# Layer 1 of a fused attention and four-matmul kernel by seven block products, with a new form of h - tanh(h)

## The chip, the cores and the metric

The kernel runs on one core of one Trainium2 chip. The metric is the device time in microseconds (us). The program's name for every instruction's line is a helper's (L215), so groups are told apart by engine, operation and shape. PE is TensorE, DVE VectorE, ACT ScalarE, POOL GpSimd, SP the engine that issues most plain DMAs.

## The reference

Sigmoid attention over 4 batches x 12 heads x 448 tokens x 64, then two feed-forward pairs on 1792 tokens, all in float32:

```
scores = q @ k.T / 8 - log(448);  x = sigmoid(scores) @ v     # -> (1792, 768)
h = x @ moe_w_in                  # layer 1, 768 -> 2048
g = h - tanh(h);  y = g @ moe_w_out        # layer 2, 2048 -> 768
b = y @ moe2_w_in                 # layer 3, 768 -> 2048
b = max(b, 0) + alpha * min(b, 0);  out = b @ moe2_w_out      # layer 4
```

## The kernel before

Matrix products are done in float16 with every operand split in a high and a low part: hi*hi + hi*lo + lo*hi, three matmuls for one (PASSES). A power of two, taken from the largest or the root mean square value (scale_of: a maximum over the free axis on DVE, over the partitions on POOL, then some ten tiny DVE instructions), scales activations into float16's range. A split is one high part (ACT or DVE) and one low part (DVE, `scalar_tensor_tensor`).

Weights come as 64-bit words. `words` turns a block of 128 x 768 into float32 by three DVE instructions, `to_scratch` splits it and stores high and low in DRAM through a POOL DMA, `fetch` loads it again through SP when PE needs it. 16 such blocks make a layer's weights.

Tokens go in two halves (sb 0 and 1) of 896 = 2 x 448. Layers 2 to 4 are done by Strassen's seven products on 2x2 blocks of weights and of activations, in the order SEQ = 1, 2, 6, 5, 7, 4, 3. `convert_quarter` makes from four blocks of weights (a quarter q of the layer) the seven sums that the products need (WSUM: by accumulating DMAs on POOL, or by DVE). `entry` makes the seven sums of activations ahead of layer 3, `exits` ahead of layers 2 and 4; `multiply_in` is one product of layer 3 (18 matmuls), `multiply_out` the seven of layers 2 and 4.

Layer 1 is a plain product: 16 blocks of output features (`product`) x two token halves, 36 matmuls each, half 1 behind half 0 by a lag. `convert` prepares its 16 blocks of weights. `bend` takes h - tanh(h) from PSUM: Tanh, then a polynomial in tanh(h)^2 (three Squares) for small h, and h - tanh(h) itself for large h, chosen by a threshold (Relu, `copy_predicated`), with the block's four PSUM reads on DVE and ACT; a last Square adds up the squares for the next scale.

The order of all instructions is written out by a planner (`Plan`): every piece of work has engines that can do it, a cost, a due time counted back from the end of PE's list, and a window; it fills each engine's in-order queue by due time. 51 slots of 128 x 896 float32 hold everything; the planner hands them out too. AHEAD, CHAIN, KEEP_*, WIN_*, LAG, SPARE_V are its parameters. PSUM is four pairs of banks.

Layer 2 of half 0 needs the scale of all its 16 blocks of h - tanh(h), and all four quarters of layer 2's weights soon after its start; layer 3 takes its quarters one after another.

Of the kernel before, what the change touches and what calls it, by code (L numbers as in the profile page):

```python
# [28 lines left out]
SW = 2.0 ** 9  # L29
ACT_EXP = 14  # L30
# [5 lines left out]
T2_MAX = 0.07960005252012954  # L36
POLY_A, POLY_B, POLY_C = 0.21126108783558653, 0.2731174600517137, 0.6519434161747253
# [192 lines left out]
def body(ctx: ExitStack, tc, qkd, vd, w1, w2, w3, w4, al, out):  # L230
# [8 lines left out]
               for m in (1, 2, 3) for pr in range(1, 8) for q in range(NQ)}  # L239
    scratch.update({u: dr_pool.tile([128, 2 * UC], F16, name=f"scr_{u}") for u in range(NU)})  # L240
# [4 lines left out]
    cst = sb_pool.tile([128, 4], F32, name="cst")  # L245
    mx = sb_pool.tile([128, 8, KF], F32, name="mx")
# [97 lines left out]
    def convert(i):  # L344
        name = f"sw:{i}"
        words(i, name, [("#scr", i - 2)] if i > 1 else ())
        to_scratch(i, name, SW)

    def convert_quarter(m, q):
# [43 lines left out]
        put(2, a12, turned)  # L393
# [8 lines left out]
    def scale_of(g, n, f0=1.0, f1=1.0, root=None, exp=ACT_EXP, sw=SW, unit=False, reads=()):  # L402
# [6 lines left out]
        def second(e):  # L409
            if root is None:  # L410
                V.tensor_scalar(c[:, 1:2], c[:, 1:2], 2.0 ** -100, None, ALU.max)
# [8 lines left out]
            V.tensor_scalar(c[:, 5:6], c[:, 2:3], 2.0 ** -exp / sw, f1, ALU.mult, ALU.mult)  # L420
            if unit:
# [4 lines left out]
                V.tensor_scalar(c[:, 7:8], c[:, 7:8], 0.5, None, ALU.mult)  # L426

        add("V", {"V": 1.3 + (0.9 if unit else 0.0)}, second, [(f"#sa{g}",), *reads], [(f"#sc{g}",)])

    def inv_of(g):  # L430
        return sc[:, g, 5:6]
# [46 lines left out]
    def values(g, u, cost):  # L478
# [19 lines left out]
        if u == 6:  # L498
            b, j = divmod(g, H // 4)
            name = f"sx{j},{b}"  # L500
            add("A", {"A": act(T2, True)}, lambda e: A.activation(two(slot(name)), full(3), AF.Copy),
                banks(3), whole(name))
# [8 lines left out]
    turn = [0]  # L511

    def product(fp, j, sb):

        k0 = turn[0] % 4
        turn[0] += 1
        p = pst[k0]
        bt = 2 * sb + j

        def x_of(k):  # L520
            return f"sX{k // 2},{bt}"

        for c in range(2):
            w = f"sW{2 * fp + c}"

            def f(e, c=c, w=w):
                wt = pair_of(slot(w)).rearrange("p a (k c) -> p a k c", k=UN)
                for k in range(KD):
                    x = hl(slot(x_of(k)))[:, :, (k % 2) * S:(k % 2 + 1) * S]
                    for n, (x1, x2) in enumerate(PASSES):  # L530
                        PE.matmul(p[:, c, 0:S], wt[:, x1, k], x[:, x2],
                                  start=k == 0 and n == 0, stop=k == KD - 1 and n == 2)

            reads = [(w, 0), *(r for k in range(KD) for r in parts(x_of(k), (0, 1)))]
            add("T", {"T": 18 * MM}, f, list(dict.fromkeys(reads)), [(f"ps{k0}", c)], lat=0.2)
        return k0

    def lagged(n, lag):
        seq, k = [], 0
        for j in range(n):  # L540
            while k < min(n, j + lag + j // 2):
                seq.append((k, 0))
                k += 1
            seq.append((j, 1))
        return seq

    def bend(fp, j, sb, k0):

        p = full(k0)
        iv = inv_of(sb)  # L550
        u, z, t = (f"s{x}{fp},{j},{sb}" for x in "uzt")
        gs = f"sG{sb},{fp // NQ},{j},{fp % NQ}"
        f = 2 * fp + j
        s1 = [(f"#sc{sb}",)]
        add("A", {"A": act(T2, True, 1)}, lambda e: A.activation(two(slot(t)), p, AF.Tanh, scale=iv),
            [*banks(k0), *s1], whole(t))
        add("A", {"A": act(T2)}, lambda e: A.activation(slot(u), slot(t), AF.Square), whole(t), whole(u))
        add("A", {"A": act(T2, ptr=1)},
            lambda e: A.activation(slot(z), slot(u), AF.Square, scale=POLY_A, bias=cst[:, 1:2]),
            whole(u), whole(z))  # L560
        add("A", {"A": act(T2, ptr=1)},
            lambda e: A.activation(slot(u), slot(u), AF.Relu, bias=cst[:, 2:3]), [], whole(u))
        add("V", {"V": vec(T2)},
            lambda e: V.scalar_tensor_tensor(two(slot(z)), two(slot(z)), POLY_C, p, ALU.subtract, ALU.mult),
            banks(k0), whole(z))
        add("A", {"A": act(T2, ptr=1)}, lambda e: A.activation(slot(z), slot(z), AF.Square, scale=iv), s1, whole(z))
        add("V", {"V": vec(T2, 1)},
            lambda e: V.scalar_tensor_tensor(two(slot(gs)), p, iv, two(slot(z)), ALU.mult, ALU.mult),
            [*banks(k0), *whole(z), *s1], whole(gs))
        add("V", {"V": vec(T2, 1)},  # L570
            lambda e: V.scalar_tensor_tensor(p, p, iv, two(slot(t)), ALU.mult, ALU.subtract),
            [*whole(t), *s1], banks(k0))
        add("V", {"V": vec(T2, 1)},
            lambda e: V.copy_predicated(two(slot(gs)), two(slot(u)).bitcast(I32), p),
            [*banks(k0), *whole(u)], whole(gs))
        add("A", {"A": act(T2, ptr=1, acc=True)},
            lambda e: A.activation(slot(z), slot(gs), AF.Square, scale=sc[:, sb, 6:7],
                                   accum_out=mx[:, 2 + sb, f:f + 1]),
            [*whole(gs), *s1], [*whole(z), (f"mx{2 + sb}", f)])
        if f == KF - 1:  # L580
            scale_of(2 + sb, KF, sc[:, sb, 6:7], sc[:, sb, 7:8], 1.0, ACT_EXP2, SW2, reads=s1)
            exits(sb, 2 + sb, "G", "Q", MOVED[0])

# [4 lines left out]
    def entry(sb):  # L588
        g = 4 + sb

        def y(e):
            return f"sy{e},{sb}"

        def h(name, k):
            return two(slot(name))[:, k]

        def t23(c):
            return f"sT{c},{sb}"

        def t4(c):  # L600
            return f"sF{c // 2 * 2},{sb}"

        def sub(out_, a, b):
            add("V", {"V": vec(S)}, lambda e: V.tensor_tensor(h(*out_), h(*a), h(*b), ALU.subtract),
                [a, b], [out_])

        for c in range(3):
            sub((t23(c), 0), (y(c + 3), 1), (y(c), 1))
            sub((y(c), 1), (y(c), 1), (y(c), 0))
            sub((t23(c), 1), (y(c + 3), 1), (y(c), 1))  # L610
            split_act(f"sO15{c},{sb}", y(c), g, window=WIN_O)
# [366 lines left out]
```

## Time and profile before

| | us |
|---|---|
| median of 3 runs | 932.58 (932.17 to 932.75) |
| the profiled execution | 931.04 |
| its span, first to last instruction | 929.3 |
| PE busy | 916.1 |
| DVE busy | 776.2 |
| ACT busy | 632.6 |
| POOL busy | 122.6 |

Busy time is the union of an engine's instructions; the mean of a group includes what overlaps with its neighbours. A window's row gives the busy time of each engine within it. Idle time ahead of a group is put down to the engine that released it.

### The profile page before, as it was taken

Reading aid. Unit: us, or ns where it says so; the run is one execution under the profiler, and the core shown is the slowest. Engines: PE = TensorE matmul, PEld = TensorE weight load, DVE = VectorE, ACT = ScalarE, POOL = GpSimd, SP = SyncE. Lnnn points to the kernel's source line nnn. Section 1 sums busy time; section 2 is a strip of 40 time slices with the busy share of each in tenths; the row PEclk is TensorE's granted clock in tenths of the full one; section 3 lists DMA queues with packets and bytes.
Section 4 is the critical chain, followed back from the end, with each engine's and each line's share of the span. In section 5 each row is a group of like instructions: output and inputs, shape, how many; then the busy total and the mean of one; then the engine's idle time right before and its main releaser. Section 6 shows DMA issues by size and latency. Waiting matters only on the chain.

```text
span 929.3 us, 13532 instructions
## 1 busy us (share of the span) xinstructions
PE 916.1 (99%) x5136; PEld 450.6 (48%) x5136; DVE 776.2 (84%) x961; ACT 632.6 (68%) x814; POOL 122.6 (13%) x207
## 2 busy tenths in 40 slices
PE   7999999999999998999999999999999999999998
PEld 2333335555555554555555555555555455555554
DVE  6788769999988999998989997798999999974300
ACT  7889869999989998645555746876773577433300
POOL 0011210123120102000023232201210000000000
PEclk9999999999999999999999999999999999999999
DMA  9983753579381337755399999867665555453431
GB/s 351 412 288 138 247 197 120 171 238 288 119 233 54 122 119 199 242 171 207 110 330 295 368 363 347 273 203 269 241 237 204 203 189 182 149 175 117 148 121 61
DMA packets 57314, 197.51 MB, mean 213 GB/s; under 512 B 7200, under 2 KB 10528, under 8 KB 57248
## 3 DMA queue, kind: packets, MB, share of 16 engines
q0 software_dynamic: 21248, 99.10, 32.5%
q1 hardware_dynamic: 36000, 97.54, 30.6%
q8 instruction: 40, 0.66, 0.3%
q14 instruction: 26, 0.21, 0.1%
HBM read 139.21 MB, written 44.83 MB: 198 GB/s over the span
## 4 chain that ended last, share of the span: by engine, by line
PE 96%; DVE 1%; ACT 1%; DMA 1%; issue 0%; SPq 0%; ACTq 0%
PE ps L215 96%; DVE slot L215 1%; ACT slot L215 1%; DMA slot<-qk 1%; DVE ps L215 0%; SPq L215 0%; ACTq L215 0%
## 5 line engine op out<-in xcount | busy, mean ns | idle before, releaser
L215 PE MATMUL ps<-slot,slot 128*128 128x448 f16 (+2 forms) x4560 | 863.3, 369 | 3.5 <-DVE slot L215 2.3
L215 PEld LDWEIGHTS <-slot 128*128 128x128 f16 (+2 forms) x4752 | 430.4, 98 | 435.7 <-issue 33.2
L215 ACT ACTIVATE slot<-slot,sc 128x896 f16<-128x896 f32 (+1 forms) x185 | 187.6, 1032 | 70.4 <-PE ps L215 34.7
L215 ACT ACTIVATE slot<-slot 128x896 f32<-128x896 f32 (+4 forms) x211 | 185.7, 895 | 72.2 <-DVE slot L215 55.6
L215 DVE SCALAR_TENSOR_TENSOR slot<-slot,sc,slot 128x896 f16<-128x896 f32 (+1 forms) x146 | 161.6, 1137 | 30.8 <-ACT slot L215 30.6
L215 DVE SCALAR_TENSOR_TENSOR slot<-slot,slot 128x768 f16<-128x768 f32 (+2 forms) x125 | 120.2, 971 | 22.1 <-ACT slot L215 18.3
L215 DVE SCALAR_TENSOR_TENSOR slot<-stage,slot 128x768 int32<-128x768 int32 x128 | 120.6, 951 | 1.0
L215 POOL DMA_DIRECT2D scr<-slot x100 | 57.8, 583 | 300.3 <-DVE slot L215 207.2
L215 ACT ACTIVATE slot<-ps 128x896 f32<-128x896 f32 (+1 forms) x76 | 59.3, 792 | 50.9 <-PE ps L215 44.2
L215 DVE SCALAR_TENSOR_TENSOR slot<-ps,sc,slot 128x896 f32<-128x896 f32 (+1 forms) x50 | 48.3, 978 | 54.2 <-PE ps L215 30.8
L215 DVE TENSOR_TENSOR slot<-slot,slot 128x896 f32<-128x896 f32 (+2 forms) x98 | 92.9, 974 | 0.3
L215 ACT ACTIVATE slot<-ps,cst 128x896 f32<-128x896 f32 x84 | 79.6, 1014 | 7.9 <-PE ps L215 7.7
L215 ACT ACTIVATE slot<-ps,sc 128x896 f32<-128x896 f32 (+1 forms) x56 | 46.9, 839 | 55.4 <-PE ps L215 55.3
L215 POOL DMA_DIRECT2D stage<-w x60 | 35.1, 585 | 253.9 <-DVE slot L215 218.7
L215 ACT ACTIVATE slot<-slot,cst 128x896 f32<-128x896 f32 x64 | 66.4, 1038 | 1.8 <-DVE slot L215 0.6
L215 PE MATMUL ps<-slot 64*128 64x448 f16 (+1 forms) x576 | 57.4, 359 | 5.7 <-ACT slot L215 5.6
L215 DVE SCALAR_TENSOR_TENSOR slot<-slot,nalpha,slot 128x448 f32<-128x448 f32 x64 | 41.6, 677 | 10.9 <-ACT slot L215 10.8
L215 DVE TENSOR_TENSOR slot<-ps,slot 128x896 f32<-128x896 f32 (+1 forms) x42 | 36.8, 884 | 5.7 <-PE ps L215 3.9
L215 DVE TENSOR_SCALAR slot<-stage 128x768 int32<-128x768 int32 x64 | 35.0, 556 | 6.7 <-PE ps L215 3.6
L215 ACT ACTIVATE junk<-slot 128x448 f16<-128x448 f32 (+1 forms) x36 | 25.4, 706 | 20.4 <-DVE slot L215 19.9
L215 POOL DMA_DIRECT2D slot<-slot x32 | 29.3, 925 | 75.3 <-DVE slot L215 48.2
L215 PEld LDWEIGHTS ps<-slot,slot 128*64 128x64 f32 (+1 forms) x384 | 20.1, 135 | 38.6 <-issue 36.4
(21 smaller groups left out, 190.8 us busy)
## 6 DMA issues: line engine op xcount, KB each, us to landing
slot<-scr SPq DMA_DIRECT2D x184, 384.0 KB, 3.7
stage<-w POOLq DMA_DIRECT2D x60, 768.0 KB, 6.3
scr<-slot POOLq DMA_DIRECT2D x100, 384.0 KB, 5.2
slot<-slot POOLq DMA_DIRECT2D x32, 384.0 KB, 7.9
slot<-qk SPq DMA_DIRECT2D x23, 448.0 KB, 9.1
slot<-v SPq DMA_DIRECT2D x12, 448.0 KB, 9.0
out_t<-slot SPq DMA_DIRECT2D x24, 224.0 KB, 2.0
stage<-w SPq DMA_DIRECT2D x4, 768.0 KB, 11.3
```

Of the source, the lines that this page charges most:

```text
L215: return lambda *args, **kw: self.tc.keep_in_program_order(f(*args, **kw))
```

## The change

- Layer 1 goes by the seven products too. `layer_in` is now one loop for layers 1 and 3: for each half, for each quarter, the products 1, (4 and 3 of the quarter before), 2, 6, 5, 7. Half 0 is finished before half 1 starts. The weights of layer 1 are made by `convert_quarter` (28 scratch blocks in place of 16; WSUM[0] is False, its sums are on DVE), and its activations by `entry(0, sb)`, whose additions go through accumulating DMAs on POOL (MOVED[0] is True). Weights of layer 1 are fetched once for each half.
- h leaves PSUM into a slot: `copy_h` (ACT) after product 1, 6, 7 or 4, `finish_h` (DVE) adds products 2, 3 or 5. `bend` then works on the slot: for small h, h times the square of arctan(1.103 tanh(0.520 h)), for large h, h - tanh(h). The threshold can go to ACT or DVE.
- Off-diagonal blocks are kept with the other sign, so that the sums before the products are additions into a block in place (`join`, `plus`); the signs are put in by copies with scale -1 and by subtractions.
- For layer 4's scale the sums of the two Relus' outputs and the largest alpha stand in for the sum of squares (`relu_b`, `steepest`), and 32 Squares of layer 3 go.
- The planner's parameters are others.

```diff
-AHEAD = {1: (0, 1, 3, 0), 2: (19, 22, 0, 20), 3: (27, 50, 7, 42)}
-CHAIN = {1: 5, 2: 1, 3: 4}
-MOVED = (False, False)
-LAG, KEEP_W, KEEP_F, KEEP_P, WIN_F, WIN_O, WIN_P, SPARE_V, WIN_Q = 4, 6, 4, 7, 16, 31, 39, 12, 51
-WSUM = (True, True, False)
+AHEAD = {0: (23, 20, 16, 16), 1: (0, 16, 12, 25), 2: (41, 32, 35, 15), 3: (0, 60, 25, 0)}
+CHAIN = {0: 7, 1: 3, 2: 5, 3: 7}
+MOVED = (True, False, False, False)
+KEEP_W, KEEP_F, KEEP_P, WIN_F, WIN_O, WIN_P, SPARE_V, WIN_Q = 7, 5, 12, 14, 43, 29, 8, 16
+WSUM = (False, True, True, False)
+PACE = (2, 3)
...
+    def bend(sb, i, j, q):
+        h, u, t = (f"s{x}{sb},{i},{j},{q}" for x in "hut")
+        z = f"sG{sb},{i},{j},{q}"
...
+        add("A", {"A": act(T2)}, lambda e: A.activation(slot(z), slot(h), AF.Tanh, scale=G_IN), whole(h), whole(z))
+        add("A", {"A": act(T2)}, lambda e: A.activation(slot(z), slot(z), AF.Arctan, scale=G_MID), (), whole(z))
+        add("A", {"A": act(T2)}, lambda e: A.activation(slot(z), slot(z), AF.Square, scale=G_OUT), (), whole(z))
+        def large(e):
+            if e == "A":
+                A.activation(slot(u), slot(z), AF.Relu, bias=cst[:, 2:3])
+            else:
+                V.tensor_scalar(slot(u), slot(z), G_MAX, None, ALU.is_gt)
+        add("AV", {"A": act(T2, ptr=1), "V": vec(T2, fast=True)}, large, whole(z), whole(u))
+        add("V", {"V": vec(T2)}, lambda e: V.tensor_tensor(slot(z), slot(z), slot(h), ALU.mult), whole(h), whole(z))
+        add("A", {"A": act(T2)}, lambda e: A.activation(slot(t), slot(h), AF.Tanh), whole(h), whole(t))
+        add("V", {"V": vec(T2)},
+            lambda e: V.tensor_tensor(slot(t), slot(h), slot(t), ALU.subtract), whole(h), whole(t))
+        add("V", {"V": vec(T2)},
+            lambda e: V.copy_predicated(slot(z), slot(u).bitcast(I32), slot(t)), [*whole(u), *whole(t)], whole(z))
...
+    def copy_h(sb, i, j, q, k0):
...
+        add("A", {"A": act(T2, True, 1)}, lambda e: A.activation(two(slot(name)), full(k0), AF.Copy, scale=iv),
+            [*banks(k0), (f"#sc{sb}",)], whole(name))
+    def finish_h(sb, i, j, q, k0):
...
+        add("V", {"V": vec(T2, 1)},
+            lambda e: V.scalar_tensor_tensor(two(slot(name)), full(k0), iv, two(slot(name)), ALU.mult, ALU.add),
+            [*banks(k0), (f"#sc{sb}",)], whole(name))
+        bend(sb, i, j, q)
...
+    def plus(out_, a, moved):
+        if moved:
+            add("G", {"G": 0.9, "M": 0.45},
+                lambda e: G.dma_start(out=half(*out_), in_=half(*a), accum_op=ALU.add), [a], [out_], lat=5.0)
...
+        for c in range(3):
+            s0, s1 = (f"sx{c},{2 * sb}", f"sx{c},{2 * sb + 1}") if m == 0 else (f"sy{c},{sb}", f"sy{c + 3},{sb}")
+            got = {}
+            if m == 0:
+                got.update(operand(f"sO{m},a{c},{sb}", s0, 1, 2))
+                plus((s0, 0), (s1, 0), MOVED[m])
+                got[5] = alone(c, s0)
+                plus((s1, 0), (s1, 1), MOVED[m])
+                got.update(operand(f"sO{m},c{c},{sb}", s1, 7, 3))
+                plus((s0, 0), (s1, 1), MOVED[m])
+                plus((s0, 1), (s0, 0), MOVED[m])
...
+            got.update(operand(f"sO{m},d{c},{sb}", s0, 6, 4))
...
-    def squares(name, into, g, col):
-        add("A", {"A": act(T2, acc=True)},
-            lambda e: A.activation(slot(into), slot(name), AF.Square, scale=SQ, accum_out=mx[:, g, col:col + 1]),
-            whole(name), [*whole(into), (f"mx{g}", col)])
+    def relu_b(out_, src, scale, sb, place, reads, ps):
+        add("A", {"A": act(T2, ps, acc=True)},
+            lambda e: A.activation(two(slot(out_)), src(), AF.Relu, scale=scale,
+                                   accum_out=mx[:, 6 + sb, place:place + 1]),
+            reads, [*whole(out_), (f"mx{6 + sb}", place)])
...
+    for m in range(4):
+        for q in range(NQ):
+            convert_quarter(m, q)
+    def layer_in(m, copied, finished, last, ended):
+        tail = []
+        for sb in range(2):
+            for q in range(NQ):
+                yk, xk, zk = q % 2, 2, 3
...
+                multiply_in(m, 1, sb, q, yk, True)
+                copied(sb, 0, 0, q, yk)
+                if tail:
+                    tail.pop(0)()
+                multiply_in(m, 2, sb, q, xk, True)
+                finished(sb, 0, 0, q, xk)
+                if tail:
+                    tail.pop(0)()
+                multiply_in(m, 6, sb, q, yk, False)
+                copied(sb, 0, 1, q, yk)
+                multiply_in(m, 5, sb, q, zk, True)
+                multiply_in(m, 7, sb, q, yk, False)
+                copied(sb, 1, 1, q, yk)
+                finished(sb, 1, 1, q, zk)
+                tail = [fourth, third]
...
+    for sb in range(2):
+        scale_of(sb, KD, root=SQ, unit=True)
+        entry(0, sb)
+    layer_in(0, copy_h, finish_h, last_h, ended_h)
     for sb in range(2):
         second_layer(sb)
+        scale_of(4 + sb, 2 * KD, 1.0, inv_of(2 + sb), SQ, reads=[(f"#sc{2 + sb}",)])
+        entry(2, sb)
+    layer_in(2, copy_b, finish_b, last_b, ended_b)
     for sb in range(2):
         fourth_layer(sb)
```

## Rows read from the trace of the kernel before

**Rows 1.** The page's busy time, share of the span and instructions of each engine.
```profile
PE 916.1 (99%) x5136; PEld 450.6 (48%) x5136; DVE 776.2 (84%) x961; ACT 632.6 (68%) x814; POOL 122.6 (13%) x207
```

**Rows 2.** Timeline of PE: start, length, count, idle time before with its releaser.
```profile
353.64 372.61 PE L215 MATMUL ps<-slot,slot 128*128 128x448 f16 x1968 [2.34 <-DVE slot L215]
727.26 197.96 PE L215 MATMUL ps<-slot,slot 128*128 128x448 f16 x1044 [1.00 <-ACT slot L215]
```

**Rows 3.** Windows: stretch, length, busy (instructions) per engine, clock, DMA share, GB/s.
```profile
core 0: us, PE busy (x) PEld busy (x) DVE busy (x) ACT busy (x) POOL busy (x), PEclk, DMA share, GB/s
0.00:11.50 11.50, 5.83 (x40) 2.19 (x41) 4.74 (x7) 7.25 (x10) 0.34 (x7) 1.00 0.82 291
...
11.50:60.00 48.50, 48.50 (x378) 16.40 (x379) 39.41 (x50) 40.92 (x49) 3.44 (x6) 1.00 0.96 375
60.00:127.50 67.50, 67.50 (x530) 22.56 (x528) 52.95 (x76) 60.24 (x73) 11.93 (x22) 1.00 0.62 217
...
542.00:640.00 98.00, 98.00 (x520) 50.69 (x518) 82.20 (x116) 69.78 (x96) 18.90 (x30) 1.00 0.84 283
...
200.00:270.00 70.00, 70.00 (x372) 36.21 (x371) 68.36 (x74) 67.90 (x85) 16.03 (x25) 1.00 0.68 204
11.50:443.50 432.00, 429.66 (x2563) 200.26 (x2563) 390.68 (x466) 363.41 (x452) 60.15 (x100) 1.00 0.61 204
131.60:349.00 217.40, 217.40 (x1151) 112.45 (x1150) 207.50 (x240) 203.31 (x247) 33.64 (x55) 1.00 0.50 158
```

**Rows 4.** Groups by form, whole span, PE: count | busy us, mean ns | idle before.
```profile
L215 PE MATMUL ps<-slot,slot 128*128 128x448 f16 x4176 | 790.8, 352 | 3.5 <-DVE slot L215 2.3 <-ACT slot L215 1.0
```

**Rows 5.** The same groups, whole span, DVE and ACT.
```profile
L215 ACT ACTIVATE slot<-slot,sc 128x896 f16<-128x896 f32 x120 | 121.2, 1035 | 67.5 <-PE ps L215 34.7 <-DMA out_t<-slot 12.1 <-DVE slot L215 10.7
...
L215 ACT ACTIVATE slot<-slot 128x896 f32<-128x896 f32 x112 | 105.5, 946 | 30.5 <-DVE slot L215 27.2 <-DMA slot<-slot 2.0
...
L215 ACT ACTIVATE slot<-slot,cst 128x896 f32<-128x896 f32 x64 | 66.4, 1038 | 1.8 <-DVE slot L215 0.6
...
L215 ACT ACTIVATE slot<-slot,sc 128x896 f32<-128x896 f32 x64 | 65.9, 1033 | 2.9 <-DVE slot L215 2.6
...
L215 ACT ACTIVATE slot<-slot 128x768 f16<-128x768 f32 x75 | 62.0, 836 | 25.2 <-DVE slot L215 15.4 <-issue 5.6 <-DMA slot<-slot 1.3
...
L215 DVE COPY_PREDICATED slot<-slot,ps 128x896 f32<-128x896 int32 x32 | 37.9, 1185 | 0.1
...
L215 DVE SCALAR_TENSOR_TENSOR ps<-ps,sc,slot 128x896 f32<-128x896 f32 x32 | 36.8, 1150 | 0.0
...
L215 DVE SCALAR_TENSOR_TENSOR slot<-ps,sc,slot 128x896 f32<-128x896 f32 x32 | 36.7, 1146 | 5.3 <-ACT slot L215 4.8 <-issue 0.3
...
L215 DVE SCALAR_TENSOR_TENSOR slot<-slot,ps 128x896 f32<-128x896 f32 x32 | 34.4, 1075 | 0.2 <-ACT slot L215 0.2
...
L215 ACT ACTIVATE slot<-ps,sc 128x896 f32<-128x896 f32 x32 | 31.9, 995 | 5.3 <-PE ps L215 5.3
...
L215 DVE TENSOR_TENSOR slot<-slot,slot 128x768 f32<-128x768 f32 x16 | 15.1, 951 | 0.1
...
L215 DVE TENSOR_SCALAR slot<-slot 128x896 f16<-128x896 f32 x17 | 10.6, 623 | 4.5 <-DMA slot<-qk 2.6 <-PE ps L215 1.7
...
L215 ACT ACT_TABLE_LOAD x1 | 1.3, 1283 | 0.7 <-PEq L970 0.7
```

**Rows 6.** Groups of DVE by form, from 0 to 443.5 us.
```profile
L215 DVE SCALAR_TENSOR_TENSOR slot<-stage,slot 128x768 int32<-128x768 int32 x68 | 64.3, 951 | 0.6
...
L215 DVE SCALAR_TENSOR_TENSOR slot<-slot,sc,slot 128x896 f16<-128x896 f32 x49 | 54.1, 1141 | 4.3 <-ACT slot L215 4.2
...
L215 DVE SCALAR_TENSOR_TENSOR slot<-slot,slot 128x768 f16<-128x768 f32 x46 | 43.4, 950 | 7.9 <-ACT slot L215 5.0 <-PE ps L215 2.2
...
L215 DVE TENSOR_TENSOR slot<-slot,slot 128x896 f32<-128x896 f32 x29 | 30.5, 1080 | 0.0
```

**Rows 7.** Timeline of DVE at the start of layer 1.
```profile
137.42 5.39 DVE L215 SCALAR_TENSOR_TENSOR slot<-slot,sc,slot 128x896 f16<-128x896 f32 x5
```

More of the change, by code (lines that the diff above doesn't have):

```diff
@@ L500, in values @@
             name = f"sx{j},{b}"
-            add("A", {"A": act(T2, True)}, lambda e: A.activation(two(slot(name)), full(3), AF.Copy),
-                banks(3), whole(name))
+            for i in range(2):
+                add("A", {"A": act(S, True)},
+                    lambda e, i=i: A.activation(two(slot(name))[:, i], p[:, i, 0:S], AF.Copy,
+                                                scale=float(sign_of(i, b % 2))),
+                    [("ps3", i)], [(name, i)])
             col = 2 * j + b % 2
@@ L538, in lagged @@
[L538 to L582, printed above, removed]
@@ L630, in f, with multiply_in @@
+    def multiply_in(m, pr, sb, q, k0, fresh):
+        p = pst[k0]
+        w = f"sv{m},{pr},{q},{sb}"
+        fetch((m, pr, q), w)
+        mine = [ops[m, sb, pr, c] for c in range(3)]
         def f(e):
@@ L639, in f, with copy_b @@
                                   skip_group_check=True)
-        add("T", {"T": 18 * MM}, f, [(w, 0), *(x for name, half in mine for x in parts(name, (half,)))],
+        add("T", {"T": 18 * MM}, f, [(w, 0), *(x for name, k in mine for x in parts(name, (k,)))],
             banks(k0), lat=0.2)
-    def copy_of(k0, name):
-        add("A", {"A": act(T2, True)}, lambda e: A.activation(two(slot(name)), full(k0), AF.Copy),
+    def copy_b(sb, i, j, q, k0):
+        name = f"sB{sb},{i},{j},{q}"
+        add("A", {"A": act(T2, True)},
+            lambda e: A.activation(two(slot(name)), full(k0), AF.Copy, scale=float(sign_of(i, j))),
@@ new lines, in finish_b, with total @@
+    def finish_b(sb, i, j, q, k0):
+        a, b = f"sB{sb},{i},{j},{q}", f"sb{sb},{i},{j},{q}"
+        plain = sign_of(i, j) > 0
+        def total(e):
+            if plain:
+                V.tensor_tensor(two(slot(a)), full(k0), two(slot(a)), ALU.add)
+            else:
+                V.tensor_tensor(two(slot(a)), two(slot(a)), full(k0), ALU.subtract)
+        add("V", {"V": vec(T2)}, total, banks(k0), whole(a))
+        place = 2 * (4 * q + 2 * i + j)
+        relu_b(b, lambda: two(slot(a)), -1.0, sb, place, whole(a), False)
+        relu_b(a, lambda: two(slot(a)), 1.0, sb, place + 1, (), False)
+        f0 = 2 * q + i * KF // 2
+        if plain:
+            leak(a, b, a, f0, ALU.add, nalpha)
+        else:
+            leak(a, a, b, f0, ALU.subtract, alpha)
@@ L770, in copied @@
         def copied(bk, row, j, last):
-            add("A", {"A": act(S, True)}, lambda e: A.activation(y_half(row, j), bank(bk), AF.Copy),
+            add("A", {"A": act(S, True)},
+                lambda e: A.activation(y_half(row, j), bank(bk), AF.Copy, scale=float(sign_of(row // 3, j))),
                 [region(bk)], [(f"sy{row},{sb}", j)])
@@ new lines, in last_h, with last_b, ended_h @@
+    def last_h(sb, i, j, q, k0):
+        copy_h(sb, i, j, q, k0)
+        bend(sb, i, j, q)
+    def last_b(sb, i, j, q, k0):
+        a, b = f"sB{sb},{i},{j},{q}", f"sb{sb},{i},{j},{q}"
+        place = 2 * (4 * q + 2 * i + j)
+        relu_b(b, lambda: full(k0), -1.0, sb, place, banks(k0), True)
+        relu_b(a, lambda: full(k0), 1.0, sb, place + 1, banks(k0), True)
+        leak(a, b, a, 2 * q + i * KF // 2, ALU.subtract, alpha)
+    def ended_h(sb):
+        scale_of(2 + sb, KF, sc[:, sb, 6:7], sc[:, sb, 7:8], reads=[(f"#sc{sb}",)])
+        exits(1, sb, "G", "Q")
@@ L853, in body, with ended_b @@
+    def ended_b(sb):
+        scale_of(6 + sb, 2 * KF, 1.0, inv_of(4 + sb), None, ACT_EXP2 + 1, reads=[(f"#sc{4 + sb}",), ("amax",)])
+        exits(3, sb, "B", "P")
     for sb in range(2):
         scale_of(sb, KD, root=SQ, unit=True)
-        for j in range(KD // 2):
-            for b in range(2 * sb, 2 * sb + 2):
-                split_act(f"sX{j},{b}", f"sx{j},{b}", sb)
-    for q in range(NQ):
-        convert_quarter(1, q)
-    got = set()
-    for n, sb in lagged(KF, LAG):
-        fp, j = divmod(n, 2)
-        for u in (2 * fp, 2 * fp + 1):
-            if u not in got:
-                got.add(u)
-                fetch(u, f"sW{u}")
-        bend(fp, j, sb, product(fp, j, sb))
```

288 lines of the change are left out of this document (115 added, 173 removed).

## The prediction, made before the result was known

> **What bounds the kernel now.** I read the page's busy shares first: TensorE (PE) is busy in 99% of a 929.3 us span, VectorE (DVE) in 84%, ScalarE (ACT) in 68% [rows 1]. Then PE's timeline: from 125.37 us to the end it runs in three blocks, and the idle time ahead of the second and the third is 2.34 us (waiting for DVE, at the start of layer 2) and 1.00 us (waiting for ACT, in layer 3) [rows 2]. Before the blocks stands the attention stage, which PE also fills from about 11.5 us on. So a product that is left out shortens the span, as long as DVE and ACT deliver operands at the new speed. The third view is busy time by stretch [rows 3]: in layer 1 (131.6 to 349) DVE has 207.5 of 217.4 us and ACT 203.3, that is 94.5% together; from 200 to 270 they have 68.36 and 67.90 of 70, or 97.3%. In layer 3 ACT has slack (69.8 of 98). So the stretch to watch is the one up to the second half of layer 2, where all of layer 1's elementwise work has to be done. PE's pitch comes from the 200-to-270 row: 70.00 us for 372 matmuls, 0.188 us each.
>
> **TensorE.** Layer 1 before is 32 products of 36 matmuls, 1152; after it is 7 products x 4 quarters x 2 halves x 18 = 1008, like layers 2 to 4 (1152 + 3 x 1008 = 4176, the count of [rows 4]). 144 x 0.188 = 27.1 us go. The 2.34 us wait at layer 2 goes too: it waits for the exit of token half 0, whose last product now stands 94 us (504 x 0.188) ahead of layer 2. I leave the 1.00 us. The sum against the profiled execution's own 931.04 us: 931.04 - 27.1 - 2.3 = 901.6 if no new wait comes. The profiled execution is 1.5 us under the median 932.58, so 903.1 in the metric.
>
> **What DVE and ACT get.** All rows are of [rows 5] unless named.
> - Weights of layer 1: 28 scratch blocks in place of 16. 12 more low parts on DVE x 0.950 [rows 6] = 11.4 us, 12 more high parts (ACT at 0.836) = 10.0; and 16 sums of 0.951 = 15.2 on DVE, since layer 1's sums are not sent to the DMA.
> - Operands of layer 1: 10.5 full-size splits per half in place of 6, 9 more in all: 9 x 1.141 [rows 6] = 10.3 on DVE, 9 x 1.035 = 9.3 on ACT. Their additions go to 24 accumulating DMAs on POOL's queue.
> - The bend, 32 times. ACT before: 0.995 + 0.946 + 2 x 1.038 + 2 x 1.033, in sum 194.7 us (the short read of each sum stays). After: a scaled copy out of PSUM (0.995), Tanh, Arctan, Square, Tanh (four of 0.946) and the summed Square (1.033): 186.0. The threshold is one more, on ACT (1.038, 33.2 in all) or on DVE (nearest row 0.623, 19.9); I take ACT. DVE before: 1.075 + 1.146 + 1.150 + 1.185, 145.8; after: 24 x 1.146 and 32 x (2 x 1.080 [rows 6] + 1.185), 134.6.
> Arctan is in no row; I take Tanh's or Square's length, one pass over 896 elements (bounds 0.946 and 1.038, the nearest forms: 3 us apart over 32).
> Sum of the rows: DVE 11.4 + 15.2 + 10.3 - 11.2 = +25.7; ACT 10.0 + 9.3 - 8.7 + 33.2 = +43.8; together 69.5 us. Neighbouring instructions overlap: five low parts of 1.14 take 5.39 us, so the pitch is 1.06, 0.93 of the row [rows 7]. 69.5 x 0.93 = 64.6 us of engine time.
>
> **Where it must fit.** The second half of layer 2 can start only when all bends, all weights of layers 1 and 2 and the exit of half 0 are done. Before, by 443.5 us, the two engines had been busy for 395.4 and 370.7 us (0 to 11.5 plus 11.5 to 443.5 [rows 3]), 766 together. Of that some was ahead of need: two of the 34 weight blocks converted (68 word operations, 46 low parts), five of the 49 operand splits with four high parts on ACT, and the 13 block sums of half 1 out of 29 [rows 6]: 4 x 0.951 + 2 x 0.950 + 5 x 1.141 + 13 x 1.080 + 4 x 1.035 = 29.6, x 0.93 = 27.5. Needed after: 766 - 27.5 + 64.6 = 803 us of two engines. The point itself stands at 353.64 + 492 x 0.188 = 446.2 before; without new waits at 446.2 - 29.4 = 416.8. 803 of 2 x 416.8 is 96.3%, against 83% before. That is as dense as the densest stretch of the trace, over the whole time, attention included, where the two engines had 205.5 of 255 us (80.6%) up to 127.5. So it doesn't quite fit, and PE will wait there, or in pieces ahead of it.
> How much: in the attention stage the extra weight work has PE's time to fill, and I put the share half way between 80.6 and 97.3%, at 89%, 227 us. The other 576 us then run at the mean of 94.5 and 97.3%, 95.9%: 576 / 1.918 = 300.3 us, so 427.8, 11.0 us late. At 97.3% it is 423.5 (6.7 late), at 94.5% 432.3 (15.5 late), and with no better attention stage and 94.5% 443.6 (26.8 late). At 97.3% throughout there is no wait. Ends of the unknown: 0 and 27; I take 11. 931.04 - 29.4 + 11.0 = 912.6, 914 in the metric.
>
> **What costs nothing.** In layer 3 the 32 Squares (0.946 each) go and 64 Relus take over the sum: ACT is at 71% there and PE at 100%, so it gains nothing. The exits' blocks in another order, the signs folded into copies and sums, the bound from alpha and the extra scale factor are a handful of short instructions early or beside busy PE: 0, and 2 us if they fell into a start of a layer. SP's queue gets 40 more fetches of 384 KB in layer 1, one per product of 3.4 us, the rate at which layer 3 runs without waiting at a DMA share of 0.84; layer 1 has 0.50 before [rows 3]. POOL's queue is in order, so an accumulating DMA that waits for x holds the weight loads and stores behind it; POOL is busy 13%, and the loads stand a block ahead. Bounds 0 and 3 us, I take 0; uncovered, a late fetch would cost its product's wait. If the wait stays, late next is the exit of half 1: its reduce, its first splits, then PE.
> TensorE's clock: it is at full (2.4 GHz) in every stretch here, that around the 2.34 us wait included [rows 3]. The Trainium skill (TensorE: Matmul & The Clock Gate, the part on the clock gate) says that a pause that is long enough throws the engine back to 1.2 GHz. By that, a wait in one piece would also slow matmuls after it, some us on top; no run here shows it yet. The sum goes without it.
>
> **Rivals.**
> 1. It fits (wait under 5 us): 901 to 908, by the row 903. For it: 200 to 270 shows both engines at 97% together, and h now leaves PSUM by one copy, so PE no longer waits for a whole bend. Against: it asks that of 400 us. Chance 0.24.
> 2. The forecast, a wait of 5 to 19 us: 908 to 922. Chance 0.45.
> 3. A wait of 19 to 27 us: 922 to 930.6, still faster. Chance 0.11. A wait of 27.5 to 31.3 us is no change: 0.04.
> 4. Slower, by overload at the middle of layer 2: the two engines hold only the share that they had from 11.5 to 443.5, 754 of 864 us or 87.3% [rows 3]. 576 / 1.746 = 329.9, so 457.4, 40.6 late: 944. It decides from 576 / (2 x (289.3 + 29.4)), under 90.4% after 127.5. For it: the in-order engines must take a copy out of PSUM between two products, 3.4 us, as they now don't have to. Against: layer 1 holds 94.5% before. Chance 0.13.
> 5. Arctan is not in the table that is loaded. The trace has one table load of 1.28 us for Sigmoid, Tanh, Square, Relu and Copy [rows 5]. If Tanh and Arctan took turns, 64 loads are 82 us more on ACT: (576 + 82) / 1.918 = 343, 470.6, 54 late: 957. Chance 0.03.
> The Trainium skill (ScalarE: Activation LUTs, Table sets: the hidden batching unit) lists sigmoid, tanh and arctan in one set. By that there is no load; no row shows Arctan.
>
> **How the numbers follow.** A measurement tells 0.2% (1.9 us) from no change. Faster: 0.24 + 0.45 + 0.11 = 0.80; same 0.04; slower 0.13 + 0.03 = 0.16. The range goes from 899 (no wait, some of the 1.00 us and the layer starts gained too) to 935, where a wait of 32 us ends: above it lies most of rivals 4 and 5, some 0.13, below it some 0.03.
>
> **What would show it.** 4032 matmuls of 128x128 with layer 1 ending about 27 us earlier; one table load; DVE and ACT both above 93% from layer 1's start to the middle of layer 2; PE's new idle time in layer 1 or at the middle of layer 2, released by DVE or ACT; 112 scratch stores in place of 100. The forecast is wrong if PE's idle time there stays under 5 us or passes 19, if it stands in layers 3 and 4, or if PE waits for DMA fetches.

## The result, and the profile after

The changed kernel takes 905.36 us (median of 4, 904.37 to 905.45), the kernel before 932.66 in the same measurement (932.17 to 932.95). The ratio is 0.9705, with a 95% interval of 0.9689 to 0.9722: faster by 27.3 us. The forecast was 914, so the direction and the removed matmuls were right and the new wait was too large: the work fits, as rival 1 (901 to 908) had it.

The profiled execution took 904.37 us, its span is 902.6. Busy time of the changed kernel, and the clock in its 40 slices (the page's first two parts):

```profile
PE 889.6 (99%) x4992; PEld 436.9 (48%) x4992; DVE 794.3 (88%) x1002; ACT 637.6 (71%) x879; POOL 156.4 (17%) x243
...
PEclk9999999999999999999999999999999999999999
```

It answers to [rows 1]: PE has 26.5 us less, DVE 18.1 more, ACT 5.0 more, in a span that is 26.7 shorter. PE's timeline (start, length, count, idle time before with its releaser) answers to [rows 2]:

```profile
315.95 37.80 PE L213 MATMUL ps<-slot,slot 128*128 128x448 f16 x199 [1.42 <-ACT slot L213]
354.33 94.18 PE L213 MATMUL ps<-slot,slot 128*128 128x448 f16 x497 [0.57 <-DVE slot L213]
449.25 250.07 PE L213 MATMUL ps<-slot,slot 128*128 128x448 f16 x1320 [0.74 <-DVE slot L213]
700.32 77.61 PE L213 MATMUL ps<-slot,slot 128*128 128x448 f16 x408 [1.01 <-ACT slot L213]
```

The 2.34 us wait is gone. New are 1.42 us (at the end of layer 1, ACT's copy), 0.57 and 0.74 us (both in layer 2, DVE); the 1.01 us in layer 3 is the old one. The three new ones add up to 2.73 us. The windows (stretch, length, busy time and instructions of each engine, clock, DMA share, GB/s) answer to [rows 3]:

```profile
core 0: us, PE busy (x) PEld busy (x) DVE busy (x) ACT busy (x) POOL busy (x), PEclk, DMA share, GB/s
0.00:11.50 11.50, 6.57 (x48) 2.95 (x48) 4.85 (x7) 7.68 (x10) 0.32 (x6) 1.00 0.82 292
11.50:60.00 48.50, 48.50 (x376) 16.20 (x368) 45.88 (x59) 44.80 (x59) 8.78 (x16) 1.00 0.97 373
60.00:127.50 67.50, 67.50 (x530) 22.63 (x528) 66.43 (x98) 66.51 (x88) 24.09 (x34) 1.00 0.98 326
...
511.00:605.00 94.00, 94.00 (x499) 48.62 (x498) 93.23 (x135) 59.55 (x96) 19.88 (x32) 1.00 0.83 289
...
127.50:416.00 288.50, 286.50 (x1518) 147.27 (x1515) 284.56 (x346) 265.96 (x354) 62.21 (x90) 1.00 0.83 258
200.00:270.00 70.00, 70.00 (x372) 36.21 (x371) 70.00 (x81) 69.22 (x90) 17.97 (x26) 1.00 0.88 262
11.50:416.00 404.50, 402.50 (x2418) 186.10 (x2411) 396.87 (x501) 377.27 (x499) 95.09 (x139) 1.00 0.87 283
```

Look at DVE first: it is busy 66.43 of 67.5 us in the second part of the attention stage, 70.00 of 70 from 200 to 270, 396.87 of 404.5 up to the middle of layer 2. ACT has 377.27 of 404.5. Both are nearly full for 400 us, and PE hardly waits. The forms up to 416 us (count | busy us, mean ns | idle before) answer to [rows 5 and 6]; DVE first:

```profile
L213 DVE TENSOR_TENSOR slot<-slot,slot 128x896 f32<-128x896 f32 x80 | 85.3, 1096 | 0.1
L213 DVE SCALAR_TENSOR_TENSOR slot<-stage,slot 128x768 int32<-128x768 int32 x72 | 67.3, 957 | 0.1
L213 DVE SCALAR_TENSOR_TENSOR slot<-slot,slot 128x768 f16<-128x768 f32 x58 | 54.7, 954 | 0.6 <-ACT slot L213 0.6
L213 DVE SCALAR_TENSOR_TENSOR slot<-slot,sc,slot 128x896 f16<-128x896 f32 x46 | 52.5, 1160 | 0.5 <-ACT slot L213 0.4
L213 DVE COPY_PREDICATED slot<-slot,slot 128x896 f32<-128x896 int32 x32 | 38.3, 1216 | 0.0
...
L213 DVE TENSOR_TENSOR slot<-slot,slot 128x768 f32<-128x768 f32 x16 | 15.2, 953 | 0.0
...
L213 DVE TENSOR_SCALAR slot<-slot 128x896 f32<-128x896 f32 x9 | 5.7, 628 | 0.0
```

```profile
L213 ACT ACTIVATE slot<-slot 128x896 f32<-128x896 f32 x128 | 115.2, 940 | 4.1 <-PE ps L213 2.2 <-DVE slot L213 1.6
...
L213 ACT ACTIVATE slot<-slot,cst 128x896 f32<-128x896 f32 x23 | 23.7, 1034 | 2.4 <-DVE slot L213 1.3 <-issue 1.0
...
L213 ACT ACT_TABLE_LOAD x1 | 1.3, 1283 | 0.7 <-PEq L972 0.7
```

The 128 passes of 0.940 us are Tanh, Arctan, Square and Tanh, 32 of each, and every one of them takes between 0.93 and 0.96 us: Arctan is as long as the others. There is still one table load, so rival 5 is out. The Trainium skill (ScalarE: Activation LUTs, Table sets: the hidden batching unit) lists sigmoid, tanh and arctan in one set; the one table load agrees. The threshold went to ACT 23 times and to DVE 9 times.

How narrow it is shows in the timeline where half 1's scale is made, in layer 2 (start, length, what, idle before):

```profile
407.67 16.62 PE L213 MATMUL ps<-slot,slot 128*128 128x448 f16 x87
...
413.01 0.17 DVE L213 TENSOR_REDUCE sc<-mx 128x1 f32<-128x16 f32 x1
...
413.97 0.76 POOL L213 PARTITION_ALL_REDUCE sc<-sc  x1
...
416.01 6.64 ACT L213 ACTIVATE slot<-slot,sc 128x896 f16<-128x896 f32 x7 [0.65 <-PE ps L213]
...
417.42 5.40 DVE L213 SCALAR_TENSOR_TENSOR slot<-slot,sc,slot 128x896 f16<-128x896 f32 x5
```

DVE finishes the reduction over half 1's blocks at 413.2 us, ACT starts the first split of half 1's exit at 416.0, and DVE the first low part at 417.4. PE goes straight on: the row from 407.67 is inside the block from 354.33, which has no gap up to 448.5. By the counts (1320 + 1044 matmuls from 449.25 on, 2016 of them in layers 3 and 4, so 348 of half 1's 504 in layer 2) PE began half 1 at about 419.2, an estimate at 0.188 us each; the first low part ended at about 418.6.

### The profile page after: what moved, and what is told of

It is laid out like the page before. It is cut to its first block, busy times and chain, and to the rows that moved or that the text cites. A ratio compares the mean times of both kernels' runs of the same rounds, so it can differ in the third digit from the quotient of the medians.

```text
span 902.6 us, 13531 instructions
## 1 busy us (share of the span) xinstructions
PE 889.6 (99%) x4992; PEld 436.9 (48%) x4992; DVE 794.3 (88%) x1002; ACT 637.6 (71%) x879; POOL 156.4 (17%) x243
## 4 chain that ended last, share of the span: by engine, by line
PE 87%; DVE 8%; ACT 2%; issue 2%; DMA 1%; POOL 0%; SPq 0%; DVEq 0%; ACTq 0%
PE ps L213 87%; DVE slot L213 8%; ACT slot L213 2%; DMA slot<-qk 1%; DVE sc L213 0%; POOL sc L213 0%; SPq L213 0%; POOL scr L213 0%; DVEq L213 0%; ACTq L213 0%
## 5 line engine op out<-in xcount | busy, mean ns | idle before, releaser
L213 PE MATMUL ps<-slot,slot 128*128 128x448 f16 (+2 forms) x4416 | 836.5, 370 | 4.1 <-ACT slot L213 2.4
L213 PEld LDWEIGHTS <-slot 128*128 128x128 f16 (+1 forms) x4608 | 416.8, 98 | 422.6 <-issue 32.8
L213 ACT ACTIVATE slot<-slot 128x896 f32<-128x896 f32 (+3 forms) x288 | 250.9, 903 | 72.6 <-DVE slot L213 54.9
L213 ACT ACTIVATE slot<-slot,sc 128x896 f16<-128x896 f32 (+2 forms) x170 | 169.9, 1020 | 95.7 <-PE ps L213 43.2
L213 DVE SCALAR_TENSOR_TENSOR slot<-slot,sc,slot 128x896 f16<-128x896 f32 (+1 forms) x160 | 174.9, 1115 | 34.6 <-ACT slot L213 34.4
L213 DVE TENSOR_TENSOR slot<-slot,slot 128x896 f32<-128x896 f32 (+2 forms) x178 | 177.2, 1018 | 0.2
L213 ACT ACTIVATE slot<-ps 128x448 f32<-128x448 f32 (+1 forms) x88 | 60.6, 709 | 32.9 <-PE ps L213 32.4
L213 POOL DMA_DIRECT2D slot<-slot x56 | 52.2, 1018 | 61.0 <-DVE slot L213 33.2
L213 DVE COPY_PREDICATED slot<-slot,slot 128x896 f32<-128x896 int32 x32 | 38.3, 1216 | 0.0
L213 DVE TENSOR_SCALAR slot<-slot 128x768 f16<-128x768 f32 (+2 forms) x50 | 28.9, 590 | 0.4 <-DMA slot<-qk 0.3
```

Source lines behind the costliest of these rows:

```text
L213: return lambda *args, **kw: self.tc.keep_in_program_order(f(*args, **kw))
```

## The experiments

Times are medians; the difference is to the changed kernel's 905.36 us, and the ratio (95% interval) to the kernel before on the same chip. The kernel before took 931.5 to 932.7 us on these chips, so a difference to 905.36 is good to some 1.5 us; where that matters the ratio is the better guide. "The planner's numbers" are AHEAD, CHAIN, KEEP_*, WIN_*, SPARE_V and PACE; an experiment leaves them as in the changed kernel where nothing else is said.

**PE's list: the matmuls put back.**

```diff
-            for i in range(2):
+            for i in range(2 if m or pr != 2 else 4):
+                i = i % 2
...
```

> Layer 1's second product is done twice, the second time from a fresh start in PSUM, so the output is the same; 144 matmuls are added, as many as the change took out. Theory A (PE's list sets the time, DVE and ACT just fit): 144 x 0.188 = 27.1 us come back, less the some 2.7 us of waits that layer 1 and 2 now show, which the longer layer covers: 929 to 933 us. Rival B (DVE and ACT set the time, and the matmuls were mostly hidden): under 915 us.

Measured 931.57 us, ratio 1.0001 (0.9992 to 1.0011): 26.2 us more (27.6 by the ratios), and the time of before. The 144 matmuls alone are worth what the change gave. Rival B is out.

**A bend that does almost nothing.** The whole body of `bend` ahead of the last Square becomes

```diff
+        add("A", {"A": act(T2)}, lambda e: A.activation(slot(z), slot(h), AF.Copy), whole(h), whole(z))
```

> The bend is cut to a copy: Tanh, Arctan, Square, the threshold, the second Tanh and DVE's three instructions are left out (32 times four or five passes of 0.94 us on ACT, three of 1.1 on DVE, some 220 us of engine time). The output is another one. Theory A: PE's list doesn't change, only the new waits in layers 1 and 2 (1.4 + 0.6 + 0.7 us) can go: 901 to 906 us. Rival B: DVE at 98% up to the middle of layer 2 is a bound, and a part of the 100 us that it loses shows: under 895 us.

Measured 902.49 us, ratio 0.9691 (0.9676 to 0.9705): 2.9 us less. Up to 416 us this kernel has

```profile
11.50:416.00 404.50, 403.40 (x2425) 186.70 (x2425) 335.67 (x441) 289.58 (x387) 103.62 (x153) 1.00 0.91 299
```

that is 61 us less on DVE and 88 less on ACT. PE's timeline from the end of layer 1 on:

```profile
316.04 381.52 PE L213 MATMUL ps<-slot,slot 128*128 128x448 f16 x2016 [1.10 <-ACT slot L213]
698.57 77.34 PE L213 MATMUL ps<-slot,slot 128*128 128x448 f16 x408 [1.00 <-ACT slot L213]
```

PE's two waits in layer 2 are gone, and the one at the end of layer 1 is still 1.10 us (1.42 in the changed kernel), so most of that one is not for want of engine time. The waits are 1.6 us shorter in all, the ratios say 1.3 us, and the intervals of the two kernels' ratios overlap: DVE and ACT cost the changed kernel 1 to 3 us, and PE's list is the bound.

**The two engines loaded a little more.** Each is one instruction of the bend twice; the output stays.

```diff
# heavy_dve: the predicated copy twice
...
+            lambda e: V.copy_predicated(slot(z), slot(u).bitcast(I32), slot(t)),
...
# heavy_act: the second Tanh twice
+        add("A", {"A": act(T2)}, lambda e: A.activation(slot(t), slot(h), AF.Tanh), whole(h), whole(t))
```

> The predicated copy of each bend is done twice: 32 x 1.13 = 36 us more on DVE, same output. Theory A: DVE has 5 us left up to the middle of layer 2, but some 30 us of high parts that it takes can go to ACT at one and a half times the price; (784 + 36) / (2 x 0.946) = 433, 15 us late, bounds 6 and 36: 911 to 941, by the row 920. Rival D (DVE is filled with work that nothing waits for yet, its 98% is no limit): 904 to 908.

> The second Tanh of each bend is done twice: 32 x 0.85 = 27 us more on ACT, same output. Theory A: ACT was idle 27 us up to the middle of layer 2, DVE 7; 784 + 27 = 811 us at a share of 94.6 to 97% puts that point 0 to 10 us late: 905 to 916. Less than the same time on DVE would cost. Rival D (neither engine is near its limit): 904 to 907.

Measured 948.17 us (ratio 1.0176, 1.0161 to 1.0192) with 36 us more on DVE: 42.8 more. And 919.94 us (0.9866, 0.9840 to 0.9892) with 27 us more on ACT: 14.6 more. Rival D is out for both engines: what they do is needed. DVE's price is above one for one, over my upper bound (941), ACT's is half, over my bound too (916).

Neither price is the engine's alone. The planner moved work: with the second Tanh ACT is busy 651.1 us, only 13.5 more than in the changed kernel, and DVE 804.5, 10.2 more. With the second copy the two engines were busy for less up to 416 us than in the changed kernel, 735 us together against 774:

```profile
11.50:416.00 404.50, 384.52 (x2295) 175.13 (x2294) 387.98 (x477) 346.78 (x447) 92.11 (x136) 0.98 0.84 271
```

So a part of the 42.8 us can be the order of the work, for which the planner's numbers were not fitted again. How large a part it is was not tried with this edit; with the old bend, below, it was.

**Where the additions ahead of layer 1 go.**

```diff
-MOVED = (True, False, False, False)
+MOVED = (False, False, False, False)
```

> The 24 additions ahead of layer 1 go from accumulating DMAs to DVE (24 x 0.61, some 13 us of DVE time with the overlap), half of them in the attention stage. Theory A: 784 + 13 = 797 at 94.6% puts the middle of layer 2 0 to 8 us late: 905 to 913. Rival E (the DMA engines, at a share of 0.97 in the attention stage and 0.92 in layer 1, are what is short): 1 to 3 us faster.

Measured 923.59 us (0.9905, 0.9876 to 0.9934): 18.2 more, for 13 us of DVE time, and over theory A's upper bound (913). Rival E (relief for the DMA engines) doesn't show: the DMA share up to 416 us falls from 0.87 to 0.78 and the kernel is slower. Two rows of PE, and the windows around them, show where more than the DVE time went:

```profile
405.45 0.35 PE L213 MATMUL ps<-slot,slot 128*128 128x448 f16 x1 [2.44 <-DVE slot L213]
411.61 19.77 PE L213 MATMUL ps<-slot,slot 128*128 128x448 f16 x89 [5.82 <-DVE slot L213]
```

```profile
394.00:405.00 11.00, 8.18 (x43) 4.09 (x42) 11.00 (x15) 11.00 (x15) 0.55 (x1) 1.00 0.40 138
405.00:416.00 11.00, 4.74 (x13) 1.87 (x13) 11.00 (x13) 10.35 (x15) 0.00 (x0) 0.59 0.12 36
416.00:425.00 9.00, 9.00 (x46) 4.54 (x45) 7.69 (x8) 7.40 (x11) 0.00 (x0) 0.93 0.27 87
425.00:436.00 11.00, 6.91 (x35) 3.30 (x34) 8.78 (x20) 9.24 (x21) 1.52 (x2) 0.92 0.55 179
436.00:445.00 9.00, 8.88 (x34) 4.03 (x34) 9.00 (x10) 5.19 (x9) 0.00 (x0) 0.71 0.22 72
```

PE waits 2.44 and then 5.82 us, and in the stretch that holds the longer wait and begins as the other ends TensorE's granted clock is 0.59 of 2.4 GHz in the mean, so partly at its lower level, 1.2 GHz. PE is busy 895.4 us in this run and 889.6 in the changed kernel, with the same 4992 matmuls: 5.8 of the 18.2 us are slower matmuls, most of it by the clock, and the rest are waits. In the changed kernel, whose longest pause after the start is 1.42 us, the clock is 1.00 in every stretch. The Trainium skill (TensorE: Matmul & The Clock Gate, the part on the clock gate) says that a pause that is long enough throws the engine back to 1.2 GHz; the trace agrees, with the 0.59 around pauses of 2.44 and 5.82 us.

**The old bend on the new layer.** The polynomial in tanh(h)^2 comes back, on the slot that holds h:

```diff
-        add("A", {"A": act(T2)}, lambda e: A.activation(slot(z), slot(h), AF.Tanh, scale=G_IN), whole(h), whole(z))
...
+        add("A", {"A": act(T2)}, lambda e: A.activation(slot(u), slot(t), AF.Square), whole(t), whole(u))
+            lambda e: A.activation(slot(z), slot(u), AF.Square, scale=POLY_A, bias=cst[:, 1:2]),
...
+            lambda e: A.activation(slot(u), slot(u), AF.Relu, bias=cst[:, 2:3]), [], whole(u))
...
+            lambda e: V.scalar_tensor_tensor(slot(z), slot(z), POLY_C, slot(h), ALU.subtract, ALU.mult),
...
```

> The seven products of layer 1 stay, the bend goes back to the polynomial in tanh(h)^2, now on the slot that holds h: one more DVE pass (the product with z minus a constant, 1.08 us, in place of a threshold that DVE takes 9 times in 32) and one more pass on ACT at 1.03 in place of 0.94, and the threshold always on ACT. 32 x 1.08 on DVE, 32 x 0.3 to 0.5 on ACT, together some 42 us of engine time. Theory A: DVE and ACT had 787 of 832 us up to 416 us, DVE 98%; needed 784 + 42 = 826 at the share of 94.6 to 97% that was reached puts the middle of layer 2 8 to 19 us late: 913 to 925 us. Rival C (the seven products alone bring the gain, the new bend is incidental): 904 to 908.

Measured 936.86 us (1.0051, 1.0034 to 1.0067): 31.5 more, and 0.5% more than the kernel before. So the seven products without the new bend gain nothing with the changed kernel's planner numbers, and rival C is out. But the cost is far over theory A's 8 to 19 us. The planner's numbers (how far each kind of work runs ahead, the widths of its windows) were those of the changed kernel, so I gave it others, found for this amount of work:

```diff
-AHEAD = {0: (23, 20, 16, 16), 1: (0, 16, 12, 25), 2: (41, 32, 35, 15), 3: (0, 60, 25, 0)}
+AHEAD = {0: (8, 18, 2, 16), 1: (0, 16, 17, 25), 2: (25, 17, 22, 24), 3: (6, 6, 22, 24)}
...
```

> The kernel with the seven products and the old polynomial, with other numbers for the planner, chosen for this amount of work (the runs before kept the changed kernel's numbers, which were chosen for another amount). With those numbers it took 936.9 us. Theory A (what DVE and ACT have left, 5 and 27 us up to the middle of layer 2, is the limit): the 42 us more of engine time cost 8 to 19 us whatever the order, 913 to 925; what was above that was order. Rival F (the order alone decides, there is capacity left): 904 to 909. Rival G (the order has no part in it): 933 to 938.

Measured 920.23 us (0.9871, 0.9848 to 0.9895): 14.9 more, inside theory A's bounds. So 16.6 of the 31.5 us were the order of the work and the clock that the waits cost, and 14.9 are what doesn't fit with these numbers. With them the seven products and the old bend are 12.4 us faster than the kernel before (932.67 in the same measurement): the products gain without the new bend too, and on top of them the new bend is worth the other 14.9 of the change's 27.3. The row from 11.5 to 416 us, of the first and of the second:

```profile
11.50:416.00 404.50, 391.06 (x2334) 178.26 (x2331) 394.06 (x483) 358.96 (x461) 91.79 (x136) 0.99 0.84 274
```

```profile
11.50:416.00 404.50, 393.64 (x2365) 180.68 (x2364) 397.29 (x484) 378.78 (x489) 89.41 (x132) 1.00 0.84 271
```

The second has 397.29 and 378.78 us, together 776; the changed kernel has 396.87 and 377.27, 774. Two kernels with 42 us between them fill the engines to the same level, 96% of 809. No run here has more over this stretch, so I take it for the ceiling, though that no order could do better is not shown; what lies above it becomes waiting time of PE.

**What should cost nothing: Squares in layer 3.** The 32 Squares and their sums come back; nothing uses them.

```diff
+        add("A", {"A": act(T2, acc=True)},
+            lambda e: A.activation(slot(b), slot(a), AF.Square, scale=SQ,
+                                   accum_out=mx[:, sb, 8 + place // 2:9 + place // 2]), ...
```

> The 32 Squares with their sums come back in layer 3 (their sums are not used, same output): 32 x 0.95 = 30 us more on ACT in a layer in which ACT has 114 us busy of 189. Theory A: nothing changes, 904 to 907. Rival: each round of layer 3 gets later handing over PSUM, since ACT is also the one that copies: 2 to 6 us slower.

Measured 906.12 us (0.9718, 0.9693 to 0.9742): 0.8 more, not to be told from none. That the new bound for layer 4's scale lets the 32 Squares go gave nothing by itself.

**Sums of layer 1's weights by DMA.** WSUM[0] is set to True.

> The 16 sums of layer 1's weights go from DVE to accumulating DMAs of 384 KB on POOL's queue, with 8 negations on ACT: DVE loses 14 us, ACT gains 6. Theory A without a DMA limit: 902 to 906, the new waits shrink. Rival E: the DMA engines are at a share of 0.97 and 0.98 up to 127 us; 16 more transfers of 384 KB in and out, 2 us each at 375 GB/s, are 34 us of all DMA engines' time that isn't there, and the weights of layer 1 come 10 to 34 us late: 915 to 940.

Measured 983.29 us (2 runs; 1.0546, 1.0504 to 1.0587): 77.9 more, far over every expectation. The cause is not settled. Three things come together: SP loads weights ahead of q and k, so that PE's first matmul starts at 10.65 us (4.63 in the changed kernel); at the start of layer 1 PE waits for operands; and in layer 2 it waits for the fetch of a block from scratch:

```profile
0.73 1.34 SPq L213 DMA_DIRECT2D stage<-w  x3
...
2.11 2.18 SPq L213 DMA_DIRECT2D slot<-qk  x4
...
10.65 0.55 PE L213 MATMUL ps<-slot 64*128 64x448 f16 x2 [10.65 <-ACT slot L213]
```

```profile
176.67 0.53 PE L213 MATMUL ps<-slot,slot 128*128 128x448 f16 x1 [20.02 <-ACT slot L213]
...
420.07 34.46 PE L213 MATMUL ps<-slot,slot 128*128 128x448 f16 x168 [11.85 <-DMA slot<-scr]
```

The first is the order that the planner gave SP's queue, not the DMA engines' doing, and the planner's numbers were not fitted again here either; how much of the rest is the DMA engines' limit (their share is 0.98 up to 127.5 us, 0.96 in the changed kernel) stays open.

**The waits that are left.** In the last quarter of half 1 no product stands between 7 and 4, which share a PSUM bank pair, so PE must wait for ACT's copy. `layer_in` takes that quarter in another order:

```diff
+                final = sb == 1 and q == NQ - 1
...
+                if final:
+                    tail.pop(0)()
+                    multiply_in(m, 6, sb, q, yk, False)
+                    copied(sb, 0, 1, q, yk)
+                    multiply_in(m, 2, sb, q, xk, True)
+                    finished(sb, 0, 0, q, xk)
+                    multiply_in(m, 7, sb, q, yk, False)
+                    copied(sb, 1, 1, q, yk)
+                    multiply_in(m, 5, sb, q, zk, True)
+                    finished(sb, 1, 1, q, zk)
```

> In the last quarter of half 1, layers 1 and 3 take their products in the order 1, 4 and 3 of the quarter before, 6, 2, 7, 5, 4, 3, so that another product stands between each pair that shares a PSUM bank (6 and 7, 7 and 4). In the changed kernel PE waits 1.42 us and 1.01 us for ACT's copy at just these places. Planner's numbers as in the changed kernel. If those waits are the hand-over of the bank: 2.4 us faster, 903. If they are DVE's and ACT's backlog, they come back elsewhere: 905 or above.

> The same order of the last quarter, with other numbers for the planner (due times, what stays free, windows). If what is left of the waits (1.42 + 0.57 + 0.74 + 1.01 us) is a matter of order only: 901.5 to 903. If DVE's 98% is the limit: 904 to 908.

> The changed kernel's order of products with other numbers for the planner only. The two waits for the bank (1.42 and 1.01 us) stay, 0.57 and 0.74 can go: 904 to 905.4. Rival: the share that DVE and ACT reach hangs on these numbers, and the time moves by 3 us or more either way.

With the planner's old numbers 913.74 us (0.9798, 0.9784 to 0.9812): 8.4 more. The two waits are gone, but others of 4.31, 2.58 and 1.42 us come up in layer 2, as expected for a backlog. With other numbers (the first entry of `AHEAD`, for one, from (23, 20, 16, 16) to (27, 20, 1, 29)) 902.20 us (0.9675, 0.9659 to 0.9691): 3.2 less. The order of the changed kernel with new numbers of its own (that entry at (19, 15, 7, 12)): 904.79 (0.9703, 0.9689 to 0.9717): 0.6 less, not to be told from none. In this third run the two waits stay, at 1.10 and 1.01 us:

```profile
315.50 108.20 PE L220 MATMUL ps<-slot,slot 128*128 128x448 f16 x570 [1.10 <-ACT slot L220]
...
699.32 197.65 PE L220 MATMUL ps<-slot,slot 128*128 128x448 f16 x1044 [1.01 <-ACT slot L220]
```

PE's timeline of the second:

```profile
337.59 68.26 PE L220 MATMUL ps<-slot,slot 128*128 128x448 f16 x360 [0.21 <-ACT slot L220]
406.40 368.00 PE L220 MATMUL ps<-slot,slot 128*128 128x448 f16 x1944 [0.56 <-ACT slot L220]
774.56 120.47 PE L220 MATMUL ps<-slot,slot 128*128 128x448 f16 x636 [0.15 <-DVE slot L220]
```

Where the changed kernel has waits of 1.42, 0.57, 0.74 and 1.01 us, 0.21 and 0.56 are left, 3.0 us less (the 0.15 stands in both kernels). The waits at the end of layers 1 and 3 go in both runs with the new order and stay in the run with new numbers only, so most of each was the hand-over of a bank. That the whole comes out faster needs numbers that fit the order. The second is the fastest kernel here; its interval just touches the changed kernel's (0.9689 to 0.9722), so the 3 us are likely but thinly shown.

## Why the prediction was right, and where it was off

- The matmuls: 144 x 0.188 = 27.1 us. The medians moved by 27.3 us, and putting 144 matmuls back costs 26.2. Right. That 27.3 lies so near 27.1 is in part luck: 2.34 us of old waiting went and 2.73 us of new came.
- The waits of before: 2.34 us gone, 1.00 us left. Right.
- The step that failed is "so it doesn't quite fit". The time lies in rival 1's range (901 to 908, chance 0.24), not in the forecast's own (908 to 922, chance 0.45), and the new idle time of 2.7 us is under the 5 us below which the prediction called itself wrong. Its other signs came, with one exception: from 127.5 to 416 us DVE is busy 98.6%, but ACT 92.2% and not above 93%.
- Durations and counts: Arctan 0.940 (taken 0.946), the products and differences of the bend 1.096 (taken 1.080), the predicated copy 1.216 (taken 1.185), 16 sums of 0.953 (taken 0.951), one table load. Right. The threshold was put on ACT; nine went to DVE.
- The term that was mis-sized is the new wait, 11.0 us, measured at 2.7. Of these only the 1.3 us in layer 2, and at most 0.3 at the end of layer 1, are for want of engine time; the other 1.1 us at the end of layer 1 are the hand-over of a bank, for which the sum had no term. The kernel before shows such a wait in layer 3, which has this order of products: the 1.00 us of [rows 2].
- How the 11.0 came about: three of its inputs can be read now. First the need, 803 us of two engines by the middle of layer 2: busy there by 416 us are 4.85 + 396.87 + 7.68 + 377.27 = 786.7, of which some 9 us are weight blocks ahead of need, and some 8 us of half 1's first splits come just after, so 786. The busy times of the groups by form up to there add up to 854 us, and the engines' busy time is 0.921 of that; before it was 766 of 817, 0.938. With that 0.938 it would be 801. Instructions that follow each other without idle time overlap more (this is read from the two traces; no run changed it by itself), and I had carried the overlap of engines that were 86% busy (766 of 887 us) over to engines at 95% (787 of 832) for everything that was already there. Second the share up to 127.5 us: 236.2 of 255, 92.6%, not 89; from 60 to 127.5 us 98.5%. Third the share after that: 95.4% (taken 95.9). By the forecast's own formula 803 with the two measured shares gives 127.5 + 567 / 1.908 = 424.6, 7.8 us late; 786 gives 415.7, in time. So the need was most of the error. The shares were measured with the smaller need, so this divides the error up and does not test its parts.
- That the two engines are what decides whether it fits was right, and the runs show it by intervention: less work gives 1 to 3 us; more work costs 14.6 to 42.8 with the planner's numbers left as they were, and 14.9 in the one case in which they were fitted again. That PE waits in the middle of layer 2 was right for the runs with more work: most of their waiting lies between 385 and 465 us.
- What costs nothing: the Squares (0.8 us, not to be told from none), right. The additions by DMA were no more than a side term in the forecast; done by DVE with the planner's numbers as they are, they cost 18.2 us.
- Rival 4 put the slower side at under 90.4% busy after 127.5 us. The old bend with unfitting numbers has (283.25 + 248.63) / 577 = 92.2% there, with 42 us more to do, and the second copy on DVE (276.11 + 235.41) / 577 = 88.7%; both came out slower than before. The mechanism exists, and the change stays clear of it.

## What to carry to other kernels

When PE's list is cut, add up what the other engines must have done by each point that PE can't pass, and compare it with the time to that point: here 786 of 833 us of two engines fitted with 3 us of waiting, and 42 us more did not, in either of the two orders tried. For a dense stretch take the pitch of back-to-back instructions, not their durations or the busy share of a stretch with idle time. When such an account is close, the order of the queues counts as much: planner numbers chosen for one kernel cost 12 and 17 us on a slightly different one (913.74 against 902.20, 936.86 against 920.23), so fit them again before judging an edit.

## What had not been expected

A microsecond more on DVE cost more than a microsecond: 36 us cost 42.8. One reason is that TensorE's clock falls among the waits. In that run PE is busy 901.6 us for the matmuls that take 889.6 in the changed kernel, with a granted clock of 0.74 between 400 and 420 us:

```profile
400.00:420.00 20.00, 10.57 (x37) 4.44 (x37) 20.00 (x21) 19.32 (x27) 2.51 (x4) 0.74 0.52 157
```

So 12 of the 42.8 us are matmuls that took longer, and some 31 are waits. Of the 12, some 2.5 are an estimate for the fifteen or so more starts after a wait (a matmul lasts 0.352 us [rows 4] where the pitch is 0.188); the rest is the clock. How much of the 42.8 us would go with planner numbers fitted to this edit is not shown; for the old bend it was 16.6 of 31.5.
